# A transformer block's hand-written instruction order, moved in small steps, with key and value products cut in two

## The chip, the cores and the metric

The kernel runs on one core of one Trainium2 chip. The metric is the device time of one execution in microseconds; the kernel before was run three times.

## The reference

A pre-layernorm block with linear attention and a dense layer, on 2048 tokens of 640 values in bf16:

```python
h  = x + A(layernorm(x));   h2 = h + B(layernorm(h))
# A: q, k, v = split(x @ wqkv), 32 heads of 20
pq = einsum("bhsd,hdf->bhsf", q, w_phi);  pk = einsum("bhsd,hdf->bhsf", k, w_phi)
phi_q = concat([softmax(pq), softmax(-pq)]);  phi_k = concat([softmax(pk), softmax(-pk)])
kv  = einsum("bhsf,bhsd->bhfd", phi_k, v);    z = sum over s of phi_k
num = einsum("bhqf,bhfd->bhqd", phi_q, kv);   den = einsum("bhqf,bhf->bhq", phi_q, z) + 1e-6
out = (num / den) @ wo
# B: silu(x @ w1) @ w2, 640 -> 1728 -> 640
```

## The kernel before

The 2048 tokens are 16 tiles of 128. One string, `ORDER`, lists every step of the program. A word such as `kp.9@0` is an operation, its token tile, and the PSUM bank it starts at; a last letter names the engine that does it (`v` VectorE, `a` ScalarE, `p` GpSimd, `s` a DMA on SyncE's queue). The loop at the end of the kernel calls `op_kp(9)` and so on in this order, and each engine runs its own instructions strictly in the order of the string. Nothing is reordered later, so the string is the schedule: waits between engines come from the data, and from PSUM banks and buffers that are used again.

The first half works tile by tile:

- `wt`, `wc` transpose the key weight in five pieces and copy them out of PSUM; `ph` forms the block-diagonal map of w_phi from `phr` and `mask5`; `fk`, `fc` fold that map into the key weight (`Wfk`), so that one product gives the mapped keys. `lq`, `gk`, `gc` do the same for the queries (`Wfq`), with a transposing DMA in place of `wt`.
- `st`, `rs` are the statistics of a token tile and 1/sqrt of its variance (the power on GpSimd); `xn` normalises the tile, and `xt`+`xc` (PE and a copy) or `xd` (a DMA) transpose it into `XnT`.
- `kp` and `vp` are the key and value products, ten matmuls of 320 columns each through `proj`; `ke` takes both exponentials of the keys on ScalarE, `kr` their sums and reciprocals on VectorE, `kn` the division (`p` all on GpSimd, `q`, `b`, `d` shared, `v` all on VectorE); `vc` copies the values out. `cc` adds the tile to the state, which stays in bank 7 until all 16 are in; `kc`, `km` then write it out masked.
- `qp`, `qs`, `qr`, `qt` are the four parts of a query product on four token tiles, and `qe` its exponentials.

The second half reads the state out: `dp` (40 small matmuls, four banks), `dw`, `dr`, `do` (weights, reciprocal, and two halves of the output `o`), `td` (a transposing DMA), `op` (output projection), `oa` (residual added), `sq`, `sr`, `hn`, `hd` (second layernorm and a transposing DMA into `HnT`), then per group of two or four tiles `up`, `ua` (first dense product, silu) and `yp`, `yh`, `yo` (second product, its last half-row, and residual with the store). `lx`, `lk`, `lv`, `lo`, `l1`, `l2`, `lh`, `lp` load tokens, weights and w_phi. `wm` are matmuls of ones, run at the start while nothing has landed.

Lines that the prediction uses: L169 and L171 are all copies out of PSUM (VectorE, ScalarE); L198 is `ph`; L236 all plain loads; L268 `wm`; L273 and L274 `st`; L278 and L281 `rs`; L297 and L302 `xn`; L308 `xt`; L322 `wt`; L337 `fk` and `gk`; L370 `proj`; L395 `ke`; L403 and L406 `kr`; L414 and L418 `kn`; L427 `cc`; L457 the query products; L479 `qe`; L504 `dp`; L539 `do`; L559 `td`; L566 `op`; L605 and L613 `hn`; L630 `hd`; L645 and L655 `up`; L691 `yp`; L704 `yh`.

Of the kernel before, what the change touches and what calls it, by code (L numbers as in the profile page):

```python
# [30 lines left out]
lx.12.16.s vp.1@6 st.10 xt.2@5 vp.0@0 xc.2.a xn.9.a vc.0.a vp.2@2 st.11 lo.2.5.s xn.3.v xt.3@4 xc.3.a  # L31
rs.10.12 xn.8.a vc.2.a vc.1.a kp.2@0 ke.2 st.4 xd.9 st.5 kp.3@4 lo.0.2.s ke.3 rs.4.6 vp.3@2 xn.11.v vp.9@6
vc.9.a xn.4.a kp.9@0 ke.9 vc.3.a st.12 st.13 st.6 rs.12.14 xd.8 kr.1 kn.1.p kp.8@4 ke.8 mc.1 xn.13.a xn.12.a
xd.11 vp.11@6 vp.8@0 vc.8.a xn.5.v kr.0 kp.11@2 lq.2.s ke.11 st.7 rs.6.8 xn.6.a st.14 st.15 rs.14.16 xd.4
kr.9 vp.4@4 vc.4.a xd.5 vp.5@0 kn.0.p vc.11.a kr.2 vc.5.a kn.9.p kp.5@2 kr.11 kn.11.p gk.2@4 xn.10.a gc.2.a
xd.12 vp.12@6 vc.12.v kr.3 kn.3.p kp.4@0 xn.15.a ke.4 kp.12@4 cc.9 cc.1 kr.4 kn.4.p cc.0 xn.14.v cc.11 ke.5
kr.5 kn.2.d xd.13 ke.12 kr.12 lq.4.s xd.6 kp.6@0 lq.0.s ke.6 vp.13@2 vc.13.a kp.13@4 ke.13 vp.6@0 xd.15
xd.10 gk.4@2 vp.10@4 vc.6.a lq.3.s gk.3@0 gc.4.a gc.3.a vc.10.a kn.5.q kp.10@2 kn.12.p kr.6 xn.7.a l1.3.s
kn.6.q lq.1.s gk.1@0 gc.1.a kr.13 kn.13.p cc.4 cc.5 l1.0.s ke.10 kr.10 cc.2 cc.3 cc.12 xd.14 xd.7 kr.8
kn.8.p kn.10.d vp.15@4 vc.15.a kp.15@0 ke.15 kp.14@2 gk.0@4 gc.0.a vp.7@0 ke.14 kr.14 kn.14.p qp.0.1@4  # L40
qs.0.1 qr.0.1 kp.7@2 ke.7 l2.10.13.s kr.15 l1.2.s cc.8 vc.7.v cc.13 l2.2.4.s cc.10 qt.0.1 qp.0.0@2 qs.0.0
kn.15.p qr.0.0 qt.0.0 qe.0.1 l2.4.6.s kr.7 kn.7.v l2.6.8.s qe.0.0 vp.14@0 vc.14.a qp.0.2@6 qs.0.2 cc.6 cc.7
mt qe.0.2 cc.15 cc.14 kc km.0 lh.s qp.3.0@4 qs.3.0 qr.3.0 km.1 dp.0@0 l1.4.s close dw.0.p dr.0 qt.3.0
do.0.1.p qe.3.0 qp.2.0@6 qs.2.0 qr.2.0 qt.2.0 qe.2.0 do.0.0.p dp.1@0 dw.1.p qp.1.0@4 dr.1 do.1.0.p qs.1.0
qr.1.0 qt.1.0 qe.1.0 qp.1.1@6 td.0 do.1.1.p td.1 dp.3@0 dw.3.p dr.3 do.3.0.p qs.1.1 qr.1.1 qt.1.1 qe.1.1
qp.3.2@4 qp.1.2@5 dp.2@0 dw.2.p qs.1.2 qe.1.2 do.3.1.p td.3 qs.3.2 op.0@6 dr.2 do.2.1.p do.2.0.p qe.3.2 oa.0
dp.4@0 dw.4.p td.2 sq.0 qp.2.2@5 qs.2.2 qe.2.2 op.1@6 oa.1 sr.0 qp.2.1@4 dp.6@0 dw.6.p l1.5.s l1.1.s qs.2.1
qr.2.1 hn.0.a hd.0 sq.1 qt.2.1 sr.1 hn.1.v hd.1 qe.2.1 op.3@6 oa.3 sq.3 dp.5@0 dw.5.p op.2@4 sr.3 oa.2
hn.3.a sq.2 dr.5 do.5.0.p do.5.1.p qp.3.1@6 qs.3.1 l2.0.2.s l2.8.10.s qr.3.1 dp.9@0 dw.9.p td.5 dr.9
do.9.0.p dr.6 do.6.1.p dr.4 do.4.1.p do.4.0.p td.4 qt.3.1 qe.3.1 up.0.2@4 ua.0.2 dp.7@0 sr.2 up.0.0@6 ua.0.0  # L50
dw.7.p dr.7 up.0.3@4 ua.0.3 do.6.0.p dp.8@0 dw.8.p dr.8 hn.2.a up.0.1@6 ua.0.1 td.6 do.8.0.p op.5@4 oa.5
dp.12@0 dw.12.p dr.12 yp.1.0@6 do.7.1.p do.7.0.p sq.5 td.7 hd.3 op.4@4 oa.4 sr.5 hn.5.v hd.5 do.9.1.p sq.4
td.9 sr.4 hn.4.a dp.10@0 dw.10.p yp.1.1 yp.0.1@4 yh.0.0 hd.2 hd.4 yo.1 dp.11@0 dw.11.p dr.11 do.8.1.p
do.11.0.p td.8 yp.0.0 yo.0 op.7@6 oa.7 sq.7 dr.10 op.6@0 oa.6 sq.6 sr.6 op.9@2 up.1.6@4 do.11.1.v td.11 oa.9
sq.9 dp.15@0 ua.1.6 sr.9 up.1.5@6 ua.1.5 up.1.1@4 hn.9.v hd.9 do.10.0.p dw.15.p dr.15 hn.6.v hd.6 op.8@6
# [12 lines left out]
"""

@with_exitstack  # L70
def kernel(
# [194 lines left out]
    def op_wm(n=512):  # L266
        one = nc.const_aps.tensor
        nc.tensor.matmul(mm1()[:, 0:n], one(1.0, (P, P), BF16), one(1.0, (P, n), BF16), start=True, stop=True)  # L268

    def op_st(t):  # L270
        stats = sm.tile([P, 2, 6], F32, name="stats")
        for k in range(2):
            nc.vector.bn_stats(stats[:, k, :], X[:, t, k * 320 : (k + 1) * 320])  # L273
        nc.vector.bn_aggr(MV[:, t, :], stats[:])  # L274

    def op_rs(a, b):
# [86 lines left out]
            tl["gk", ce][:, 1, 0:320].rearrange("p (k r f) -> p k r f", k=2, r=C),  # L363
        )

    def proj(t, W):
        ps = mm2()
        for c in range(C):
            for half in range(2):
                nc.tensor.matmul(  # L370
                    ps[:, half, 0:320], tok(XnT[t // GT], t)[:, c, :], W[:, c, half * 320 : (half + 1) * 320],
                    start=(c == 0), stop=(c == C - 1),
                )
# [384 lines left out]
```

## Time and profile before

| | us |
|---|---|
| median of three runs | 236.25 (236.18 to 236.31) |
| the profiled execution | 236.35 |
| its span in the profile | 234.4 |
| TensorE busy | 230.5 |
| VectorE, ScalarE, GpSimd busy | 133.5, 114.5, 95.4 |

The span is from the first to the last instruction of the profile; some 2 us of the execution lie around it. Times in the rows are from the start of the span. A row of a timeline gives the start, the busy time, the engine, the line, the operation, out<-in with shapes, the count of merged instructions, and in brackets the idle time before it and what ended it. A piece of the chain of waits gives start, length, engine and line. A row of the grouped view ends with busy time, the mean of one in ns, and the idle time before the group. A DMA row gives the size and the median time from issue to landing. A matmul's row counts its way through the array, so that matmuls that follow each other overlap in it; their pace is read from starts, or from the pieces of the chain.

### The profile page before, as it was taken

How to read it: one execution, taken by the hardware profiler on the slowest of the kernel's cores; microseconds unless marked ns; L12 is line 12 of the kernel's file. 1: busy time of each engine (PE TensorE's matmuls, PEld its weight loads, DVE VectorE, ACT ScalarE, POOL GpSimd, SP SyncE). 2: the span in 40 equal slices, each digit the busy share in tenths (PEclk: the TensorE clock that was granted, in tenths of full speed). 3: DMA queues.
4: the chain of work that ended last, by engine and by line, in shares of the span. 5: the costliest groups of instructions: out<-in, count | busy, mean ns of one | idle time of the engine just before them, and what ended most of it. 6: DMA issues, size and time to landing. Idle time of an engine off the chain costs nothing.

```text
span 234.4 us, 6307 instructions
## 1 busy us (share of the span) xinstructions
PE 230.5 (98%) x2674; PEld 148.4 (63%) x2674; DVE 133.5 (57%) x249; ACT 114.5 (49%) x171; POOL 95.4 (41%) x190
## 2 busy tenths in 40 slices
...
DMA packets 44844, 20.67 MB, mean 88 GB/s; under 512 B 34448, under 2 KB 44304, under 8 KB 44816
## 3 DMA queue, kind: packets, MB, share of 16 engines
...
## 4 chain that ended last, share of the span: by engine, by line
PE 98%; ACT 1%; DVE 0%; issue 0%
PE mm L691 24%; PE mm L645 24%; PE mm L370 19%; PE mm L457 10%; PE mm L566 9%; PE mm L504 3%; PE mm L268 2%; PE mm L427 2%; PE mm L337 1%; PE mm L655 1%; PE mm L704 1%; ACT EqT L479 1%; PE mm L322 1%; PE mm L308 0%; DVE ob L721 0%
## 5 line engine op out<-in xcount | busy, mean ns | idle before, releaser
L691 PE MATMUL mm<-w,shT 128*128 128x320 bf16 (+2 forms) x416 | 58.7, 299 | 0.0
L645 PE MATMUL mm<-HnT,w 128*128 128x512 bf16 (+1 forms) x325 | 58.6, 337 | 0.0
L691 PEld LDWEIGHTS <-shT 128*128 128x128 bf16 x416 | 39.6, 98 | 17.2 <-issue 1.1
L667 ACT ACTIVATE shT<-mm 128x1024 bf16<-128x1024 f32 (+2 forms) x29 | 27.6, 963 | 44.6 <-PE mm L645 43.1
L712 DVE TENSOR_TENSOR ob<-mm,X 128x640 bf16<-128x640 f32 x15 | 12.3, 819 | 62.3 <-PE mm L691 59.3
L645 PEld LDWEIGHTS <-w 128*128 128x128 bf16 x325 | 31.4, 98 | 23.2
L370 PEld LDWEIGHTS <-XnT 128*128 128x128 bf16 x320 | 30.8, 98 | 12.0
L414 POOL TENSOR_TENSOR Ek<-Ek,Sk 128x1280 bf16<-128x1280 bf16 (+2 forms) x15 | 32.9, 2217 | 4.0 <-DVE Sk L406 4.0
L539 POOL TENSOR_TENSOR o<-u,rd 128x320 bf16<-128x320 f32 x28 | 19.9, 727 | 22.9 <-DVE rd L533 16.4
L583 ACT ACTIVATE sq<-X 128x640 bf16<-128x640 bf16 x16 | 11.7, 732 | 28.3 <-DVE X L575 27.2
L566 PE MATMUL mm<-wo,ot 128*128 128x320 bf16 x160 | 23.9, 299 | 0.3 <-ACT EqT L479 0.3
L457 PE MATMUL mm<-XnT,Wfq 128*128 128x512 bf16 x100 | 23.8, 380 | 0.0
L370 PE MATMUL mm<-wv,XnT 128*128 128x320 bf16 x160 | 23.7, 299 | 0.0
L370 PE MATMUL mm<-Wfk,XnT 128*128 128x320 bf16 x160 | 23.5, 299 | 0.0
L395 ACT ACTIVATE Ek<-mm 128x640 bf16<-128x640 f32 x32 | 20.5, 714 | 6.0 <-PE mm L370 5.1
L403 DVE TENSOR_REDUCE Sk<-Ek 128x64 f32<-128x1280 bf16 x16 | 23.2, 1452 | 0.3 <-ACT Ek L395 0.3
L479 ACT ACTIVATE EqT<-mm 128x1024 bf16<-128x1024 f32 (+1 forms) x24 | 19.7, 879 | 4.9 <-PE mm L457 4.8
L575 DVE SCALAR_TENSOR_TENSOR X<-mm,X 128x640 bf16<-128x640 f32 x16 | 13.0, 818 | 15.4 <-PE mm L566 15.1
L566 PEld LDWEIGHTS <-ot 128*128 128x128 bf16 x160 | 15.7, 98 | 7.3 <-issue 0.2
L273 DVE BATCH_NORM_STATS2 stats<-X 128x6 f32<-128x320 bf16 x32 | 13.6, 467 | 3.8 <-DMA X<-in_A_x_dram 3.8
L457 PEld LDWEIGHTS <-Wfq 128*128 128x128 bf16 x100 | 9.1, 98 | 9.3
L525 DVE TENSOR_TENSOR u<-mm,w 128x672 f32<-128x672 f32 x16 | 13.7, 857 | 1.2 <-DVE w L523 0.3
...
## 6 DMA issues: line engine op xcount, KB each, us to landing
out_dram<-ob SPq DMA_DIRECT2D x15, 160.0 KB, 1.8
...
wk<-in_A_wqkv_dram SPq DMA_DIRECT2D x4, 160.0 KB, 4.2
...
```

Of the source, the lines that this page charges most:

```text
L370: nc.tensor.matmul(ps[:, half, 0:320], tok(XnT[t // GT], t)[:, c, :], W[:, c, half * 320 : (half + 1) * 320], start=(c == 0), stop=(c == C ...
L395: nc.scalar.activation(Ek[:, s, :].rearrange("p (a n) -> p a n", a=2), tl["kp", t][:, :, 0:320], AF.Exp, scale=1.0 - 2.0 * s,)
L403: nc.vector.tensor_reduce(Sk[:], tl["ek", t][:].rearrange("p s (h f) -> p (s h) f", f=DH), axis=AX.X, op=ALU.add,)
L414: nc.gpsimd.tensor_tensor(Ek3[:, 0:n], Ek3[:, 0:n], Sk[:, 0:n].unsqueeze(2).to_broadcast([P, n, DH]), op=ALU.mult,)
L457: nc.tensor.matmul(tl["qp", g, i][:, k, :], Wfq[:, c, r * P : (r + 1) * P], XnT[g][:, c, :], start=(c == 0), stop=(c == C - 1),)
L479: nc.scalar.activation(E[:, s, rs[0] : rs[-1] + 1, :], tl["qp", g, i][:, 0 : len(rs), :], AF.Exp, scale=1.0 - 2.0 * s,)
L525: nc.vector.tensor_tensor(u[:], A[1][:, :, :, 0:21], w[:].unsqueeze(3).to_broadcast([P, 4, 8, 21]), op=ALU.mult,)
L539: (nc.vector if eng == "v" else nc.gpsimd).tensor_tensor(tl["o", t][:, a * 320 : (a + 1) * 320].rearrange("p (h f) -> p h f", f=DH), tl["u ...
L566: nc.tensor.matmul(ps[:, half, 0:320], tl["ot", t][:, c, :], wo[:, c, half * 320 : (half + 1) * 320], start=(c == 0), stop=(c == C - 1),)
L645: nc.tensor.matmul(ps[:, i * W : (i + 1) * W], w1[:, c, fc * P : (fc + 1) * P], HnT[g][:, c, 0:W], start=(c == 0), stop=(c == C - 1), skip ...
L667: nc.scalar.activation(sh[:, a:b], tl["up", g, k][:, 0 : b - a], AF.Silu)
L691: nc.tensor.matmul(ps, shT[g][:, fc * W + i * P : fc * W + (i + 1) * P], w2[:, fc, a:b], start=first and fc == 0, stop=last and fc == FC - ...
```

## The change

All 622 words of `ORDER` are written anew as 670. The steps are the same ones, with these differences:

- `kp` and `vp` are cut in two: `kp`, `vp` do three of the five weight pieces (six matmuls), new words `kq`, `vq` the other two (four). A product's second part can stand behind other work.
- `st` is cut in two: new word `sa` does the first half of a tile's statistics, `st` the second half and the aggregate.
- The fifth piece of the key weight (`wt.4`) is transposed second, and the state products `cc` are grouped otherwise.
- `ph` goes from VectorE to GpSimd, behind the constants of the values (`mo`) and the mask (`mk`).
- Copies: `wc` 4, 2 on ScalarE and 0, 1, 3 on VectorE (before 0, 1 and 2, 3, 4); `xc.2` to VectorE, `vc.7`, `vc.12` to ScalarE; `xn` 2, 9, 12, 15 to VectorE and 3, 11, 14 to ScalarE; `hn` 5, 7, 8, 10, 11, 13, 14 to ScalarE and 3 to VectorE; eight halves of `do` from GpSimd to VectorE and two the other way; `kn` 2, 7, 10 to GpSimd alone, 5 shared half and half, 12 and 14 with a quarter on GpSimd.
- The loads of `wo` go from the first 18 us to behind `xd.14`; `l1` and `l2` stand in another order, and `lh` goes behind `td.7`.
- PSUM banks are given out anew; the read-outs `dp` use banks 4 to 7 where most used 0 to 3.

The start, and the parts of the order that the prediction speaks of:

```diff
-mk mo lx.0.1.a lk.0.1.s lp.a lx.1.2.s lk.4.5.a wm.512@7 wm.512@7 wm.512@7 wm.512@7 wm.512@7 wm.512@7
-wm.512@7 wm.512@7 wt.0@0 lk.1.2.s ta wc.0.a wm.256@2 wm.256@2 wm.256@2 wm.256@2 wm.256@2 wm.256@2 wt.1@1 wc.1.a st.0 rs.0.1
-ph.v fk.0@2 fc.0.a st.1 lk.2.3.s wt.2@4 wc.2.v lk.3.4.s wt.3@5 wc.3.v fk.1@6 fc.1.a rs.1.2 fk.2@0 fc.2.a
-lx.2.4.s xn.0.v lx.8.12.s wt.4@4 wc.4.v lv.0.3.s fk.3@2 fc.3.a xt.0@5 xn.1.v xc.0.v st.2 fk.4@6 fc.4.a
-rs.2.3 lv.3.5.s mc.0 xt.1@4 xc.1.a st.9 st.8 rs.8.10 lx.4.8.s st.3 rs.3.4 kp.0@0 ke.0 xn.2.a kp.1@2 ke.1
...
+lx.0.1.a sa.0 lk.0.1.s mo lp.a wm.512@7 wm.512@7 wm.512@7 wm.512@7 wm.512@7 wm.512@7 wm.512@7 wm.512@7
+wt.0@0 lx.1.2.s lk.4.5.a lk.1.2.s st.0 lk.2.3.s lk.3.4.s wm.256@2 wm.256@2 wm.256@2 wm.256@2 wm.256@2
+wm.256@2 wt.4@1 wt.1@2 mk ph.p rs.0.1 sa.1 st.1 ta wc.4.a wt.2@3 wc.2.a rs.1.2 lx.2.4.s wc.0.v fk.0@4 fc.0.a
+wt.3@6 wc.1.v fk.1@0 lx.8.12.s fk.2@2 xn.0.v xt.0@7 wc.3.v fk.3@4 xn.1.v fc.1.a lv.0.3.s xt.1@6 fc.2.a
+xc.0.v kp.0@0 sa.2 xc.1.a st.2 fk.4@2 fc.3.a sa.3 rs.2.3 st.3 kp.1@6 rs.3.4 xn.2.v fc.4.a kq.0 kq.1 lv.3.5.s
+ke.0 xt.2@4 sa.8 vp.0@2 vq.0 sa.9 vp.1@0 vq.1 st.8 st.9 rs.8.10 xc.2.v vp.2@4 vq.2 ke.1 sa.10 st.10 lx.4.8.s
...
+qp.0.0@0 ke.15 qs.0.0 l2.10.13.s qr.0.0 qt.0.0 qe.0.0 kr.13 kp.7@4 kq.7 kn.10.p cc.5 cc.10 xd.14 kn.4.p cc.4
+kp.14@0 kq.14 kr.12 ke.7 qp.0.1@4 qs.0.1 qr.0.1 kn.13.p cc.13 kr.15 cc.6 kn.15.p vc.15.a cc.15 ke.14 kn.12.d
+cc.12 vp.14@2 vq.14 qt.0.1 kr.7 kn.7.p cc.9 cc.7 kr.14 kn.14.d vc.14.a cc.14 qe.0.1 mt close qp.0.2@6 qs.0.2
+qp.2.0@0 kc km.0 qp.3.0@2 qs.3.0 km.1 qe.0.2 dp.0@4 l1.1.s qr.3.0 dw.0.p qt.3.0 qs.2.0 qr.2.0 l1.3.s qt.2.0
...
+dw.4.p qp.2.2@2 qs.2.2 qe.2.2 op.1@0 oa.1 td.3 qp.2.1@2 do.2.1.p td.2 sr.0 hn.0.a dp.6@4 l2.2.4.s hd.0
+qs.2.1 qr.2.1 sq.1 qt.2.1 qe.2.1 dw.6.p op.3@0 l1.4.s sr.1 hn.1.v hd.1 l2.0.2.s oa.3 sq.3 sr.3 dp.5@4 dw.5.p
+op.2@2 oa.2 dr.5 l2.4.6.s do.5.1.p qp.3.1@0 qs.3.1 qr.3.1 do.5.0.p dp.9@4 td.5 sq.2 qt.3.1 qe.3.1 dw.9.p
...
+do.8.0.p do.6.1.v op.5@2 oa.5 sq.5 do.7.0.p td.7 dp.12@4 dw.12.p dr.12 op.4@0 oa.4 lh.s yp.1.0@2 do.8.1.p
+td.8 dp.10@4 do.9.0.v yp.1.1 yp.0.1@0 td.6 sr.5 hn.5.a dw.10.p hd.5 yh.0.0 sq.4 yo.1 sr.4 dp.11@4 dw.11.p
...
+yp.14.0 yo.14 yp.15.1 yo.15 yp.13.0 yz.13.0.s yp.13.1 yz.13.1.a
...
+    def op_sa(t):
+        tl["stats", t] = sm.tile([P, 2, 6], F32, name="stats")
+        nc.vector.bn_stats(tl["stats", t][:, 0, :], X[:, t, 0:320])
+
     def op_st(t):
-        stats = sm.tile([P, 2, 6], F32, name="stats")
-        for k in range(2):
-            nc.vector.bn_stats(stats[:, k, :], X[:, t, k * 320 : (k + 1) * 320])
+        stats = tl["stats", t]
+        nc.vector.bn_stats(stats[:, 1, :], X[:, t, 320:D])
         nc.vector.bn_aggr(MV[:, t, :], stats[:])
...
-    def proj(t, W):
-        ps = mm2()
-        for c in range(C):
+    def proj(t, W, ps, cs):
+        for c in cs:
             for half in range(2):
...
     def op_vp(t):
-        tl["vp", t] = proj(t, wv)
+        tl["vp", t] = mm2()
+        proj(t, wv, tl["vp", t], range(3))
+
+    def op_vq(t):
+        proj(t, wv, tl["vp", t], range(3, C))
...
     def op_kp(t):
-        tl["kp", t] = proj(t, Wfk)
+        tl["kp", t] = mm2()
+        proj(t, Wfk, tl["kp", t], range(3))
+
+    def op_kq(t):
+        proj(t, Wfk, tl["kp", t], range(3, C))
```

More of the change, by code (lines that the diff above doesn't have):

```diff
@@ L31 @@
[L31 to L55, printed above, removed]
@@ new lines @@
+xc.0.v kp.0@0 sa.2 xc.1.a st.2 fk.4@2 fc.3.a sa.3 rs.2.3 st.3 kp.1@6 rs.3.4 xn.2.v fc.4.a kq.0 kq.1 lv.3.5.s
+ke.0 xt.2@4 sa.8 vp.0@2 vq.0 sa.9 vp.1@0 vq.1 st.8 st.9 rs.8.10 xc.2.v vp.2@4 vq.2 ke.1 sa.10 st.10 lx.4.8.s
+xn.9.v sa.11 st.11 vc.0.a sa.4 xn.3.a rs.10.12 mc.0 vc.1.a xn.8.a lx.12.16.s sa.12 xt.3@6 xc.3.a sa.7 kp.2@2
+kq.2 ke.2 xd.9 xd.8 vp.3@0 kp.3@6 lq.2.s xn.11.a kq.3 st.4 ke.3 vq.3 vc.3.a xd.11 vc.2.a kp.9@2 lq.3.s kq.9
+sa.5 sa.6 kp.8@6 st.5 rs.4.6 vp.8@0 xn.4.a vq.8 ke.9 sa.13 st.13 st.12 rs.12.14 xn.10.a xn.5.v vc.8.a st.6
@@ new lines @@
+st.7 mc.1 vp.9@4 kp.11@2 vq.9 kr.2 xn.12.v rs.6.8 xn.13.a xd.5 kq.11 ke.11 vc.9.a kn.2.p kr.3 kn.3.p vp.11@0
+kq.8 vq.11 ke.8 vc.11.a vp.5@2 vq.5 xn.6.a xd.4 vp.4@4 vq.4 kr.0 kn.0.p vc.5.a kr.1 xd.12 vc.4.a xn.7.a
+gk.2@6 kp.12@0 kq.12 vp.12@2 vq.12 gc.2.a kp.5@4 sa.14 kq.5 cc.0 vc.12.a st.14 cc.2 ke.12 xd.6 kp.6@2 vp.6@0
+vq.6 ke.5 vc.6.a kn.1.p kp.4@4 kq.6 kq.4 lq.0.s gk.0@0 cc.1 kr.11 kn.11.p ke.6 cc.11 kr.8 kn.8.p cc.8 ke.4
+sa.15 st.15 rs.14.16 kr.5 kn.5.b cc.3 kr.9 kn.9.p gc.0.a xd.10 l1.0.s kp.10@2 kq.10 ke.10 xd.13 xn.14.a
@@ new lines @@
+qp.2.0@0 kc km.0 qp.3.0@2 qs.3.0 km.1 qe.0.2 dp.0@4 l1.1.s qr.3.0 dw.0.p qt.3.0 qs.2.0 qr.2.0 l1.3.s qt.2.0
+dr.0 do.0.0.p dp.1@4 dw.1.p lo.0.2.s qe.3.0 dr.1 do.0.1.p do.1.0.p do.1.1.p qe.2.0 qp.1.0@2 qs.1.0 qr.1.0
+qt.1.0 qe.1.0 qp.1.1@0 lo.2.5.s dp.3@4 dw.3.p dr.3 do.3.1.p do.3.0.p qs.1.1 qr.1.1 l1.5.s qt.1.1 qp.1.2@2
+qp.3.2@3 dp.2@4 dw.2.p dr.2 qs.3.2 qs.1.2 qe.1.1 qe.1.2 td.0 op.0@0 td.1 oa.0 qe.3.2 sq.0 dp.4@4 do.2.0.p
+dw.4.p qp.2.2@2 qs.2.2 qe.2.2 op.1@0 oa.1 td.3 qp.2.1@2 do.2.1.p td.2 sr.0 hn.0.a dp.6@4 l2.2.4.s hd.0
@@ new lines @@
+qs.2.1 qr.2.1 sq.1 qt.2.1 qe.2.1 dw.6.p op.3@0 l1.4.s sr.1 hn.1.v hd.1 l2.0.2.s oa.3 sq.3 sr.3 dp.5@4 dw.5.p
+op.2@2 oa.2 dr.5 l2.4.6.s do.5.1.p qp.3.1@0 qs.3.1 qr.3.1 do.5.0.p dp.9@4 td.5 sq.2 qt.3.1 qe.3.1 dw.9.p
+dr.4 do.4.1.p l2.8.10.s do.4.0.p td.4 dr.9 up.0.2@2 ua.0.2 dp.7@4 l2.6.8.s dw.7.p up.0.0@0 ua.0.0 sr.2
+hn.2.a up.0.3@2 hn.3.v dp.8@4 hd.3 dr.6 do.6.0.v ua.0.3 up.0.1@0 dr.7 do.7.1.p dw.8.p hd.2 ua.0.1 dr.8
+do.8.0.p do.6.1.v op.5@2 oa.5 sq.5 do.7.0.p td.7 dp.12@4 dw.12.p dr.12 op.4@0 oa.4 lh.s yp.1.0@2 do.8.1.p
@@ new lines @@
+td.8 dp.10@4 do.9.0.v yp.1.1 yp.0.1@0 td.6 sr.5 hn.5.a dw.10.p hd.5 yh.0.0 sq.4 yo.1 sr.4 dp.11@4 dw.11.p
+dr.11 do.11.1.v yp.0.0 op.6@2 oa.6 hn.4.a do.9.1.p td.9 op.8@4 op.7@6 oa.8 sq.6 sr.6 op.9@2 oa.7 hd.4
+do.12.0.v sq.8 sr.8 hn.6.v hd.6 oa.9 yo.0 do.11.0.v sq.9 td.11 up.1.5@4 ua.1.5 sr.9 hn.9.v hd.9 hn.8.a sq.7
+sr.7 hn.7.a hd.7 dp.14@0 up.1.2@6 up.1.1@4 ua.1.1 ua.1.2 dw.14.p dr.14 up.1.3@0 ua.1.3 dr.10 up.1.6@2
+do.10.0.v do.14.1.v dp.15@4 up.1.4@0 ua.1.6 ua.1.4 dw.15.p dr.15 hd.8 up.2.6@2 ua.2.6 do.12.1.p dp.13@4
```

26 lines of the change are left out of this document (12 added, 14 removed).

## The prediction

> **What bounds the kernel now.** I read the page first (span, busy shares), then the chain of work that ended last, then the timelines of single engines over the first 13 us, where alone TensorE (PE) is not full.
>
> ```profile
> span 234.4 us, 6307 instructions
> PE 230.5 (98%) x2674; PEld 148.4 (63%) x2674; DVE 133.5 (57%) x249; ACT 114.5 (49%) x171; POOL 95.4 (41%) x190
> ...
> 4.94 1.28 PE mm L268 x6
> 6.25 0.45 PE mm L322 x5
> 6.70 0.32 PE mm L337 x6
> 8.96 0.28 PE mm L308 x5
> 38.20 1.32 PE mm L427 x128
> 45.38 1.36 PE mm L370 x10
> 65.20 1.13 PE mm L427 x128
> 68.37 2.91 PE mm L457 x13
> 71.68 2.70 PE mm L457 x12
> ...
> 88.29 1.52 PE L566 MATMUL mm<-wo,ot 128*128 128x320 bf16 x10 [0.27 <-ACT EqT L479]
> ```
>
> The first two lines are the page's, the rest are pieces of the chain, and the last is from PE's timeline. The chain is matmuls nearly from end to end, at their own pace: ten of 320 columns take 1.36 us, 136 ns each. So an order can win only where PE waits, or by fewer changes of tile shape, and it can lose wherever a producer comes late. The last line holds the only wait of PE for an engine after the start, 0.27 us. What can be won is this and part of the first 10 us.
>
> **The start.** Up to the second key product the same matmuls stand in both orders: five transposes of the key weight (wt), five products with the block map (fk), two token transposes (xt), two key products. Before, all are issued by 12.72:
>
> ```profile
> 1.70 0.56 ACTq L236 DMA_DIRECT2D wk<-in_A_wqkv_dram  x1
> wk<-in_A_wqkv_dram ACTq DMA_DIRECT2D x1, 160.0 KB, 4.3
> 5.00 0.15 DVE L278 TENSOR_SCALAR RS<-MV 128x1 f32<-128x1 f32 x1
> 5.08 0.99 DVE L198 TENSOR_TENSOR phb<-phr,mask 128x800 bf16<-128x800 bf16 x1
> 7.33 0.89 DVE L169 COPY wTk<-mm 128x640 bf16<-128x640 bf16 x2 [0.22 <-PE mm L322]
> 8.20 0.44 DVE L297 TENSOR_SCALAR xn<-X,MV,RS 128x640 bf16<-128x640 bf16 x1
> 9.45 0.48 DVE L169 COPY XnT<-mm 128x640 bf16<-128x640 bf16 x1
> 6.74 0.69 ACT L171 COPY wTk<-mm 128x640 bf16<-128x640 bf16 x1 [1.07 <-PE mm L322]
> 7.33 3.17 ACT L171 CAST Wfk<-mm 128x640 bf16<-128x640 f32 x5
> 12.72 0.71 PE L370 MATMUL mm<-wv,XnT 128*128 128x320 bf16 x4
> ```
>
> VectorE's queue led to 10 us: statistics, block map (0.99), three weight copies, two normalisations, XnT at 9.45 to 9.93. After, the map leaves VectorE and the copies stay three (pieces 0, 1, 3). With the statistics of token 1 at 5.1 in place of the map, wc.0 comes at 6.3, wc.1 6.8, xn.0 7.25, wc.3 7.7, xn.1 8.15, xc.0 8.6 to 9.1, a gain of 0.85 at most. The fifth piece lands at 1.70 + 4.3 = 6.0, 0.25 ahead of piece 1, and takes PE from the warm-up there; pieces 1 and 2 follow, and fk.0 can go at 6.85, when wc.0 is done.
>
> ScalarE then holds the end: wc.4 (at 6.0 + 0.49, the distance from 6.25 to 6.74), wc.2, fc.0, fc.1, fc.2, xc.1, fc.3, fc.4. At 0.59 a weight copy (6.74 to 7.33), 0.61 an fc (3.17 over five) and 0.6 for xc.1, fc.4 ends at 6.5 + 1.2 + 3.05 + 0.6 + 0.1 = 11.45. As the products are cut after three of five weight pieces, kp.0 needs only fc.2 and starts at 9.2 to 9.9; fk.4 (0.32), kp.1 and the first part of kq.0 fill the time to fc.4. The last 0.27 of kq.0 and the 0.54 of kq.1 come after it, so PE is through at 12.3, or 12.8 if the normalisations come late. The floor is PE without a pause from 6.0: 4 x 0.28 + 5 x 0.33 + 2 x 0.28 + 2 x 1.36 = 6.05, so 12.1. Against 12.72: **-0.6 to +0.1, I take -0.2**, as three engines have to meet.
>
> The map on GpSimd has no row. The nearest, with those of its input:
>
> ```profile
> 1.22 0.45 ACTq L236 DMA_DIRECT2D phr<-in_A_w_phi_dram  x1
> phr<-in_A_w_phi_dram ACTq DMA_DIRECT2D x1, 25.0 KB, 3.6
> L414 POOL TENSOR_TENSOR Ek<-Ek,Sk 128x960 bf16<-128x960 bf16 x2 | 3.9, 1942 | 0.0
> L414 POOL TENSOR_TENSOR Ek<-Ek,Sk 128x320 bf16<-128x320 bf16 x2 | 2.4, 1178 | 0.0
> ```
>
> On the line between 320 and 960 columns, 800 make 1.75 us, from 4.9 (1.22 + 3.6, and a start) to 6.65, 0.2 ahead of need. Between 1.2 and 1.95 by the two rows themselves, it is late by nothing that matters. Queued behind it on GpSimd are the powers for tokens 0 and 1, and xn.0 waits for the first; that is the 12.8 above.
>
> **Tile shapes.** One matmul more in a stretch of L457 costs 0.21 (2.91 against 2.70), so 12 are 2.52 and 0.18 is left for entering and leaving small tiles. The state products (cc) stood in four groups, of which the first and the last are quoted (L427); read off the new order they make five: 0+2, 1+11+8+3, 5+10+4, 13+6+15+12, 9+7+14. The read-outs (dp) and half-row groups (yh) keep their count. **+0.2.** The cuts of kp, vp and the statistics add no instruction: 0.
>
> **The wait at 88 us stays.** The new order has again qt.2.1, op.3, dp.5, then op.2 in the banks that qe.2.1 frees (2 in place of 4): 0 taken, -0.27 at best.
>
> **12 to 68 us.** The products rotate through PSUM banks that ScalarE frees. It gets two value copies more, one token copy and one xn less, so no new load. The tightest place is the end. From the end of qt.0.0 to the last state product, cc.14, PE has 3 x 1.36 of products, 2.15 of query work, nine cc at 0.28 (1.13 for four) and three entries into small tiles of 0.2: 9.3 in all. The chain beside it:
>
> ```profile
> 60.65 1.94 ACT L479 ACTIVATE EqT<-mm 128x1024 bf16<-128x1024 f32 x2 [0.32 <-PE mm L457]
> 59.03 1.30 ACT L395 ACTIVATE Ek<-mm 128x640 bf16<-128x640 f32 x2 [2.43 <-PE mm L370]
> L403 DVE TENSOR_REDUCE Sk<-Ek 128x64 f32<-128x1280 bf16 x16 | 23.2, 1452 | 0.3 <-ACT Ek L395 0.3
> L406 DVE RECIPROCAL Sk<-Sk 128x64 f32<-128x64 f32 x16 | 8.8, 553 | 0.6
> L414 POOL TENSOR_TENSOR Ek<-Ek,Sk 128x1280 bf16<-128x1280 bf16 x11 | 26.9, 2456 | 4.0 <-DVE Sk L406 4.0
> 55.45 3.14 POOL L414 TENSOR_TENSOR Ek<-Ek,Sk 128x1280 bf16<-128x1280 bf16 x1 [1.42 <-DVE Sk L406]
> ```
>
> 0.3 (a matmul's end to the next engine) + 1.94 (qe.0.0) + 1.30 (ke.7) + 2.0 (kr.7) + 2.46 (kn.7, now on GpSimd) + 1.18 (GpSimd's quarter of kn.14) = 9.2, on time by 0.1. With a kn of 3.14 it is 0.6 late. **0 to +0.6, I take +0.1.**
>
> **After 68 us** the read-out stage repeats the old order with its banks mirrored (dp in 4 to 7 in place of 0 to 3). Net six hn move from VectorE to ScalarE, and net six halves of do from GpSimd to VectorE, about one short operation there for another.
>
> ```profile
> L613 ACT ACTIVATE hn<-X,hm 128x640 bf16<-128x640 bf16 x6 | 5.5, 921 | 8.1 <-POOL hm L610 8.1
> 83.47 1.15 SPq L236 DMA_DIRECT2D w<-in_B_w_dram  x2
> 103.80 1.76 SPq L559 DMA_TRANSPOSE ot<-o  x1
> w<-in_B_w_dram SPq DMA_DIRECT2D x2, 80.0 KB, 5.6
> 110.00 0.38 PE mm L704 x4
> ```
>
> ScalarE: 6 x 0.92 = 5.5 us, hidden by PE's products, as ScalarE is busy only 49%; uncovered, each hn would cost its 0.92. On SyncE's queue the wo loads leave the first 18 us for a place behind xd.14, far ahead of op.0: 0. The fourth w1 slice now stands between hd.0 and hd.1 and may hold hd.1, which token group 0 awaits, by one issue: 0 to 0.57. The tail load lh goes behind td.7 (103.8 and one transpose, so 105) and lands by 110.6 at the latest; yh.0.0 asks for it at 110.0: 0 to 0.6. I take 0 for both, as each has other loads' company in its long row and little here. The last two projections and stores are unchanged: 0.
>
> **Sum.** -0.2 + 0.2 + 0.1 = +0.1. The profiled execution has a span of 234.4 in 236.35, so 234.5 and 236.45; the median of the runs, 236.25, lies 0.1 below it: **236.3**.
>
> **Rivals.** *Slower: the map holds VectorE's port.* While GpSimd forms the map from two SBUF tiles (4.9 to 6.65), VectorE's small add for RS at 5.0, and all queued behind it, would wait.
>
> ```profile
> 14.11 0.72 POOL L281 TENSOR_TENSOR RS<-RS,nhalf 128x2 f32<-128x2 f32 x1
> 14.21 0.15 DVE L278 TENSOR_SCALAR RS<-MV 128x1 f32<-128x1 f32 x1
> 40.24 0.77 DVE L297 TENSOR_SCALAR xn<-X,MV,RS 128x640 bf16<-128x640 bf16 x1
> ```
>
> Against: that add ran in 0.15 inside a GpSimd operation. For: an xn took 0.77 in place of 0.44 while GpSimd normalised keys. If all is held to 6.65, XnT is ready at 10.6 and PE through the set at 10.6 + 0.32 + 2.72 = 13.65, 0.9 later; with the tile shapes +1.1, **237.4**. It decides once the add waits more than 0.7.
>
> The Trainium skill ("SBUF — State Buffer", Who interferes with whom) has the shared port pair locked for a whole instruction, the other engine fully blocked. By that rule 237.4 would come out; the rows at 14 us speak against it for so small an add.
>
> I give this rival 0.15, and a late producer elsewhere (cc.14, hd.1, lh) at +0.6, 236.9, another 0.15.
>
> *Faster: PE runs without a pause from 6.0 and ScalarE is early at 88 us.* -0.6 + 0.2 - 0.27 = -0.7: **235.6**. For it: the early fifth piece, and VectorE relieved by 1 us. Against: ScalarE's eight copies follow each other without slack. Chance 0.24.
>
> **Numbers.** The forecast's case, within 0.2% (0.47 us, about what a measurement of this kernel can tell from no change), has 0.46; slower by more 0.30; faster by more 0.24. The range runs from the faster rival's 235.6 to just under the port rival, 237.3; beyond its ends lie about half of the faster case's chance and half of the port's.
>
> **What would show it.** Right: the first value product begins at 12.3 to 12.8, the stretch of L457 behind the first dp (68.37 before) within 0.5 of its old time, five L427 groups in the chain, and a wait near 0.3 at 88. The port: the second token's statistics after 6 us and the first key product after 10.3. The prediction is wrong if PE waits more than 0.5 us in one place after 13 us, or if the first 13 us gain over 0.6.

## Result and profile after

| | us | against the kernel before |
|---|---|---|
| before, median of 11 runs | 236.27 (236.13 to 236.6) | |
| after, median of 11 runs | 236.96 (236.61 to 238.2) | 1.0029, 95% interval 1.0018 to 1.0041 |
| profiled execution after | 237.15, span 235.4 | before 236.35, span 234.4 |

The change costs 0.69 us, 0.29%: inside the range, but outside the 0.2% of the forecast's own case. Of the profile after, first the page's head, then pieces of its chain of waits (start, length, what), then the waits of PE for other engines and transfers (total, times, longest):

```profile
span 235.4 us, 6297 instructions
PE 228.6 (97%) x2655; PEld 148.1 (63%) x2674; DVE 130.7 (56%) x247; ACT 119.2 (51%) x177; POOL 95.1 (40%) x192
```

```profile
1.72 4.77 DMA wk<-in_A_wqkv_dram
6.53 1.01 PE mm L327 x15
...
58.19 1.31 ACT Ek L406 x2
59.59 1.50 DVE Sk L414
61.11 0.56 DVE Sk L417
61.83 1.82 POOL Ek L425
63.65 0.49 issue
64.14 1.65 POOL Ek L425
65.84 0.38 PE mm L438 x32
...
69.47 2.75 PE mm L468 x12
```

```profile
PE mm L327 <- DMA wk<-in_A_wqkv_dram: 0.9, 1, 0.9
...
PE mm L577 <- ACT EqT L490: 0.3, 1, 0.3
```

The line numbers moved: L327 is `wt` (322 before), L374 `proj` (370), L438 `cc` (427), L468 the query products (457), L414 and L417 `kr`, L425 and L429 `kn`, L577 `op` (566), L656 `up` (645). PE shows 2655 of 2674 matmuls, so the page's 97% is a little low, and gaps of a whole matmul are missing records, not waits. Eleven of the missing ones are query matmuls (L468, 89 of 100), among them the first one behind the last state product and the first one behind the first read-out.

The stretch behind the first read-out (`dp`) starts at 69.47, against 68.37 before: 1.1 later, of which some 0.2 is a missing first record. The read-out itself starts 0.96 later (68.84 against 67.88, rows below), and the span is 1.0 longer. So all of it is lost before 69 us and nothing after. Two places show in the chain. PE waits at the start for the fifth key piece, and the end of the state stage hangs on the key chain: exponential (L406), sum and reciprocal on VectorE (L414, L417), two divisions on GpSimd (L425), last state product (L438). Before, the chain ran through matmuls here. (The 0.49 of "issue" is the rest of tile 7's division: GpSimd's timeline has it from 61.83 to 64.18.)

### The profile page after: what moved, and what is told of

Its sections match the earlier page's. It is cut to its first block, busy times and chain, and to the rows that moved or that the text cites. A ratio compares the mean times of both kernels' runs of the same rounds, so it can differ in the third digit from the quotient of the medians.

```text
span 235.4 us, 6297 instructions
## 1 busy us (share of the span) xinstructions
PE 228.6 (97%) x2655; PEld 148.1 (63%) x2674; DVE 130.7 (56%) x247; ACT 119.2 (51%) x177; POOL 95.1 (40%) x192
## 4 chain that ended last, share of the span: by engine, by line
PE 82%; DVE 9%; ACT 3%; DMA 2%; POOL 1%; issue 1%; ACTq 0%; DVEq 0%; POOLq 0%
PE mm L702 24%; PE mm L656 24%; PE mm L374 10%; PE mm L577 9%; PE mm L468 7%; DVE Sk L414 5%; PE mm L515 3%; DMA wk<-in_A_wqkv_dram 2%; DVE Sk L417 2%; ACT Ek L406 2%; POOL Ek L425 1%; DVE Ek L429 1%; PE mm L666 1%; PE mm L715 1%; PE mm L342 1%
## 5 line engine op out<-in xcount | busy, mean ns | idle before, releaser
L656 PE MATMUL mm<-HnT,w 128*128 128x512 bf16 (+1 forms) x318 | 58.3, 336 | 0.4
L656 PEld LDWEIGHTS <-w 128*128 128x128 bf16 x325 | 31.3, 98 | 23.8 <-issue 0.2
L723 DVE TENSOR_TENSOR ob<-mm,X 128x640 bf16<-128x640 f32 x15 | 12.3, 824 | 59.7 <-PE mm L702 48.6
L374 PEld LDWEIGHTS <-XnT 128*128 128x128 bf16 x320 | 30.6, 98 | 12.1 <-issue 0.4
L425 POOL TENSOR_TENSOR Ek<-Ek,Sk 128x1280 bf16<-128x1280 bf16 (+3 forms) x16 | 34.4, 2173 | 3.3 <-DVE Sk L417 3.2
L550 POOL TENSOR_TENSOR o<-u,rd 128x320 bf16<-128x320 f32 x22 | 16.0, 745 | 28.0 <-DVE rd L544 20.2
L414 DVE TENSOR_REDUCE Sk<-Ek 128x64 f32<-128x1280 bf16 x16 | 23.2, 1452 | 2.9 <-ACT Ek L406 2.9
L374 PE MATMUL mm<-Wfk,XnT 128*128 128x320 bf16 x160 | 24.5, 299 | 0.0
L374 PE MATMUL mm<-wv,XnT 128*128 128x320 bf16 x160 | 24.0, 299 | 0.2 <-issue 0.2
L577 PE MATMUL mm<-wo,ot 128*128 128x320 bf16 x160 | 23.4, 299 | 0.3 <-ACT EqT L490 0.3
L468 PE MATMUL mm<-XnT,Wfq 128*128 128x512 bf16 x89 | 22.0, 379 | 1.2 <-issue 1.0
L406 ACT ACTIVATE Ek<-mm 128x640 bf16<-128x640 f32 x32 | 20.6, 707 | 2.8 <-PE mm L374 2.6
L577 PEld LDWEIGHTS <-ot 128*128 128x128 bf16 x160 | 15.6, 98 | 7.0 <-issue 0.2
L624 ACT ACTIVATE hn<-X,hm 128x640 bf16<-128x640 bf16 x12 | 10.9, 918 | 11.2 <-POOL hm L621 11.1
L468 PEld LDWEIGHTS <-Wfq 128*128 128x128 bf16 x100 | 9.1, 98 | 9.5
```

The source lines that it names most:

```text
L374: nc.tensor.matmul(ps[:, half, 0:320], tok(XnT[t // GT], t)[:, c, :], W[:, c, half * 320 : (half + 1) * 320], start=(c == 0), stop=(c == C ...
L406: nc.scalar.activation(Ek[:, s, :].rearrange("p (a n) -> p a n", a=2), tl["kp", t][:, :, 0:320], AF.Exp, scale=1.0 - 2.0 * s,)
L414: nc.vector.tensor_reduce(Sk[:], tl["ek", t][:].rearrange("p s (h f) -> p (s h) f", f=DH), axis=AX.X, op=ALU.add,)
L425: nc.gpsimd.tensor_tensor(Ek3[:, 0:n], Ek3[:, 0:n], Sk[:, 0:n].unsqueeze(2).to_broadcast([P, n, DH]), op=ALU.mult,)
L468: nc.tensor.matmul(tl["qp", g, i][:, k, :], Wfq[:, c, r * P : (r + 1) * P], XnT[g][:, c, :], start=(c == 0), stop=(c == C - 1),)
L550: (nc.vector if eng == "v" else nc.gpsimd).tensor_tensor(tl["o", t][:, a * 320 : (a + 1) * 320].rearrange("p (h f) -> p h f", f=DH), tl["u ...
```

## Experiments

All times are medians with the ratio to the kernel before in runs on the same chip, and the 95% interval of the ratio; the changed kernel itself stands at 1.0029 and, repeated, 1.0027. Of all variants only k2, k4 and e5 have intervals clear of the changed kernel's (1.0018 to 1.0041), so everything smaller rests on the profiles, one for each variant.

### The kernel once more

> The changed kernel once more, nothing altered: a second profile of it. If the time behind the prediction lies in the order itself, the ratio is 1.002 to 1.004 again, the fifth key piece is awaited until about 6.5 us, the five groups of small-tile products return, and the pauses inside the group at 41.9 us (0.43 us), in the second matmul of the last value product (0.33) and before the last state product (0.29) return at the same places within 0.1 us. If those pauses are chance (a transfer, code arriving late), at least one of them is gone or elsewhere by more than 0.2 us and the ratio moves with it.

237.04 us, 1.0027 (1.0013 to 1.004). PE's timeline, repeated kernel first, then after (start, busy, bracket: idle before and for what):

```profile
6.01 1.28 PE L327 MATMUL mm<-ident,wk 128*128 128x128 bf16 x15
...
12.51 0.44 PE L313 MATMUL mm<-ident,xn 128*128 128x128 bf16 x5
...
68.36 0.47 PE L515 MATMUL mm<-KVBD,EqT 32*128 32x44 bf16 x40
```

```profile
6.53 1.01 PE L327 MATMUL mm<-ident,wk 128*128 128x128 bf16 x15 [0.93 <-DMA wk<-in_A_wqkv_dram]
...
12.76 0.44 PE L313 MATMUL mm<-ident,xn 128*128 128x128 bf16 x5
...
68.84 0.47 PE L515 MATMUL mm<-KVBD,EqT 32*128 32x44 bf16 x40
```

This time the fifth piece was there when the warm-up ended at 6.01, and the set of transposes, folds and key products was through at 12.51, not 12.76. So half of the 0.52 by which the piece came late in the first profile was chance that reached the end. From there to the read-out both take about the same, 55.85 and 56.08; before it took 55.16 (from 12.72 to the row below, PE's timeline of before). That part, 0.7 to 0.9 longer, belongs to the order.

```profile
67.88 0.49 PE L504 MATMUL mm<-KVBD,EqT 32*128 32x44 bf16 x40
```

### The start: which piece first

```diff
-wt.4@1 wt.1@2        (k1)      -lp.a ... lk.4.5.a       (k2)
+wt.1@2 wt.4@1                  +... lk.4.5.a lp.a
```

> Only the order of two transposes of the key weight is turned: piece 1, which landed at 6.18 us, ahead of the fifth, which landed at 6.49. Theory A, the start is bound by PE, which stands in order behind the late piece: PE leaves the warm-up at 6.2, and all behind it is 0.28 us earlier (time 0.3 below the changed kernel's). Theory B, the start is bound by ScalarE's eight copies, of which the first needs the fifth piece in either order (6.5 + 0.49): the last of the products' copies still ends at 11.9, the two key products still end at 12.7 to 12.8, and the time is the changed kernel's within 0.1 us.

> Only the load of the fifth key piece goes ahead of that of the feature weight on ScalarE's queue, about 0.5 us earlier. If its late landing is what cost the forecast gain, it lands by 6.0, ScalarE's first copy starts at about 6.5 in place of 7.0, the two key products end at 12.2 to 12.4 in place of 12.76, and the time falls by 0.3 to 0.5 us against the changed kernel. The price could be the map, whose input then lands up to 0.6 later: if the map ends after 7.0, the first product with it is late and the gain is under 0.15. If the landing does not matter, the time stays within 0.1 us.

Piece 1 first: 237.0 us, 1.0027 (1.0015 to 1.0038), no gain. It doesn't decide between its theories, as in its profile no piece was late. The fifth piece's load ahead: 238.1 us, 1.0069 (1.0057 to 1.0082). The price named came in full, and more:

```profile
6.49 1.52 POOL L200 TENSOR_TENSOR phb<-phr,mask 128x800 bf16<-128x800 bf16 x1 [2.13 <-DMA phr<-in_A_w_phi_dram]
8.06 0.47 PE L342 MATMUL mm<-phb,wTk 128*128 128x140 bf16 x6 [1.32 <-POOL phb L200]
```

With the load of w_phi behind that of the fifth piece on ScalarE's queue the map starts at 6.49 in place of 4.66, and PE waits 1.32 us for it. The piece was never the only thing that the start hung on.

### The map back on VectorE, and the cut undone

```diff
-mk ph.p rs.0.1        (k4)     -xc.0.v kp.0@0 sa.2 xc.1.a st.2 fk.4@2 fc.3.a ... fc.4.a kq.0 kq.1     (e10)
+mk ph.v rs.0.1                 +xc.0.v fk.4@2 fc.3.a fc.4.a sa.2 kp.0@0 kq.0 xc.1.a ... kp.1@6 kq.1
```

> Only the block map goes back from GpSimd to VectorE, where it took 0.99 us before. If GpSimd's map does not hold VectorE up, as the profile suggests (the small add ran in 0.15 us at 4.95, inside the map's 1.52), VectorE's first seven steps come about 1 us later: the first key product starts 0.4 to 0.9 us later than 9.72, and the time rises by 0.3 to 0.9 us against the changed kernel. If GpSimd's map held VectorE's port (the slower rival of the forecast), taking it away from GpSimd gives time back: equal or up to 0.5 us faster.

> Undoes the cut of the first two key products: as before, the fourth and fifth folded pieces and both their copies come ahead of the whole first key product, and the copy of the second token behind them. If the cut earns what the forecast says (the first part needs three of five pieces), the first key product starts about 1.2 us later (11.4 to 11.9 in place of 9.5 to 9.7), the two key products end 0.6 to 1.2 us later, and the time rises by 0.4 to 1.2 us. If PE would have been bound elsewhere, below 0.2.

The map on VectorE: 237.86 us, 1.0059 (1.0045 to 1.0073). The rows are those of this kernel, then two of the kernel after:

```profile
5.08 0.95 DVE L200 TENSOR_TENSOR phb<-phr,mask 128x800 bf16<-128x800 bf16 x1
7.77 0.49 PE L342 MATMUL mm<-phb,wTk 128*128 128x140 bf16 x6 [0.66 <-DVE wTk L171]
10.04 0.99 PE L374 MATMUL mm<-Wfk,XnT 128*128 128x320 bf16 x6
```

```profile
4.66 1.52 POOL L200 TENSOR_TENSOR phb<-phr,mask 128x800 bf16<-128x800 bf16 x1 [0.30 <-DMA phr<-in_A_w_phi_dram]
4.95 0.15 DVE L283 TENSOR_SCALAR RS<-MV 128x1 f32<-128x1 f32 x1
5.02 0.48 DVE L274 BATCH_NORM_STATS2 stats<-X 128x6 f32<-128x320 bf16 x1
```

VectorE's weight copy is late by 0.66 and the first key product starts 0.3 to 0.6 later than in the two profiles of the change. With the map on GpSimd, VectorE's add took its 0.15 us and a statistics step 0.48 inside the map's 1.52. The slower rival falls: in this profile GpSimd's map held nothing up.

The cut undone: 237.22 us, 1.0042 (1.0029 to 1.0055), some 0.2 to 0.3 us more than with the cut, less than expected and within the intervals. In its profile the key products began at 9.82 all the same, as their first matmuls need only the first pieces, and PE waited inside them for the later copies:

```profile
9.82 3.07 PE L374 MATMUL mm<-Wfk,XnT 128*128 128x320 bf16 x20
12.73 0.44 PE L313 MATMUL mm<-ident,xn 128*128 128x128 bf16 x5
```

The products end at 12.73. With the cut, in the four profiles that had no piece late and the same start (the repeat, e5, e7 and e11), they end at 12.31 to 12.52: the cut earns 0.2 to 0.4.

### The end of the state stage

```diff
-kr.7 kn.7.p cc.9 cc.7 kr.14 kn.14.d vc.14.a cc.14 qe.0.1 mt close
+kr.7        cc.9 cc.7 kr.14         vc.14.a cc.14 qe.0.1 mt close       (e6)
+mt kr.7 kn.7.p cc.9 cc.7 kr.14 kn.14.v vc.14.a cc.14 qe.0.1 close       (e8)
```

> Leaves out the division of key tiles 7 and 14 by their sums (kn.7 and kn.14); everything else stays. Theory A, the end of the state stage is bound by the key chain (exponential, sum, division on GpSimd, the last quarter): from the start of the last value product to the end of the last state product PE took 3.80 us in every profile so far, of which 0.68 is pause; without the two divisions it takes 3.1 to 3.2 and the time falls by 0.6 to 0.7 us, to the kernel before. Theory B, the pauses are PE's own (instructions that come late): the 0.2 to 0.66 us in the second matmul of the last value product stays, only the rest goes, and the time falls by 0.1 to 0.4.

> The division of key tile 14 goes wholly to VectorE (GpSimd had a quarter of it, queued behind the division of tile 7), and the transposition of the mask goes ahead of it into a pause of VectorE. Chain now: GpSimd's quarter ends 1.65 us after tile 7's division. If GpSimd is the late one, the last state product starts 0.15 to 0.5 us earlier and the time falls by as much. If VectorE alone is slower with the whole tile (1.92 us for 1280 columns once before, against 1.47 for 960 now), it starts at the same time within 0.1 us or later, and nothing is gained.

Without the two divisions 236.55 us, 1.0015 (1.0002 to 1.0028); with the last one on VectorE 236.86, 1.0024 (1.0012 to 1.0037). (e6 leaves out two divisions, so its output is not the block's; it only prices the chain.) PE's timeline from the last value product to the first read-out, parts of it, after, then e6, then e8:

```profile
62.57 0.31 PE L374 MATMUL mm<-wv,XnT 128*128 128x320 bf16 x1
63.05 1.38 PE L374 MATMUL mm<-wv,XnT 128*128 128x320 bf16 x9 [0.17 <-issue]
65.01 0.66 PE L438 MATMUL mm<-Ek,Vp 128*21 128x40 bf16 x64
65.84 0.38 PE L438 MATMUL mm<-Ek,Vp 128*21 128x40 bf16 x32 [0.17 <-POOL Ek L425]
66.37 1.46 PE L468 MATMUL mm<-XnT,Wfq 128*128 128x512 bf16 x6 [0.16 <-issue]
...
68.84 0.47 PE L515 MATMUL mm<-KVBD,EqT 32*128 32x44 bf16 x40
```

```profile
62.35 1.66 PE L374 MATMUL mm<-wv,XnT 128*128 128x320 bf16 x10
...
68.14 0.47 PE L515 MATMUL mm<-KVBD,EqT 32*128 32x44 bf16 x40
```

```profile
62.01 1.62 PE L374 MATMUL mm<-wv,XnT 128*128 128x320 bf16 x10
65.03 0.37 PE L438 MATMUL mm<-Ek,Vp 128*21 128x40 bf16 x32 [0.16 <-DVE Ek L429]
...
68.03 0.47 PE L515 MATMUL mm<-KVBD,EqT 32*128 32x44 bf16 x40
```

From the first row of each to its last: 6.27, 5.79 and 6.02; in the repeat it is 6.27 too (62.09 to 68.36). So the key chain costs 0.48, and 0.25 of that goes when VectorE takes the whole of tile 14. The 3.80 of the expectation, and the 0.47 that e11's expectation takes from e8, are too large by one matmul: they run to the first query row, and in the profile of after that row lacks its first record (11 query matmuls are listed up to the read-out, 12 in e6 and e8). In e7, e9 and e10, where the record is there, the same stretch is 3.57 to 3.58, against 3.09 in e6 (62.35 to 65.44) and 3.33 in e8.

The medians fell by 0.4 and by 0.1 to 0.2, near the 0.48 and 0.25 and less than the 0.6 to 0.7 that the first theory named. The pause inside the value product (63.05, 0.34 behind its place) cost nothing in after: it varies from 0.1 to 0.7 between the profiles, and with the chain as in after the stretch stays 6.26 to 6.32, since PE has to wait at product 14 anyway.

Why the chain is longer than forecast shows in GpSimd's quarters of a tile. The first two rows are the two of the kernel before, the others tile 14 in after, GpSimd's quarter and VectorE's part:

```profile
58.55 0.72 POOL L414 TENSOR_TENSOR Ek<-Ek,Sk 128x320 bf16<-128x320 bf16 x1
43.19 1.64 POOL L414 TENSOR_TENSOR Ek<-Ek,Sk 128x320 bf16<-128x320 bf16 x1
64.14 1.64 POOL L425 TENSOR_TENSOR Ek<-Ek,Sk 128x320 bf16<-128x320 bf16 x1
63.73 1.47 DVE L429 TENSOR_TENSOR Ek<-Ek,Sk 128x960 bf16<-128x960 bf16 x1
```

The quarter takes 0.72 when VectorE divides nothing meanwhile, and 1.64 when it does (VectorE's division ran from 42.91 to 44.24 beside the one at 43.19). A whole tile on GpSimd shows the same: 2.35 alone, 3.27 in after at 57.02, where VectorE's division of another tile ran until 58.08. In each case the one that starts second is longer by about the time that the other still runs: GpSimd's quarter at 64.14 by 0.92, with 1.06 of VectorE's division left.

### Small matmuls in a row

```diff
-kq.5 cc.0 vc.12.a st.14 cc.2 ke.12 ... vq.6 ke.5 vc.6.a kn.1.p kp.4@4 kq.6 kq.4 lq.0.s gk.0@0 cc.1 kr.11 ... cc.3
+kq.5      vc.12.a st.14      ke.12 ... vq.6 ke.5        kn.1.p kp.4@4 kq.6 kq.4 lq.0.s cc.0 vc.6.a cc.2 cc.1 kr.11 ... cc.3 gk.0@0   (e5)
+kq.5 cc.0 vc.12.a kn.1.p st.14 cc.2 cc.1 ke.12 ... vq.6 ke.5 vc.6.a   kp.4@4 kq.6 kq.4 lq.0.s gk.0@0      kr.11 ... cc.3   (e9)
```

> State products 0 and 2 move behind the products of token 6 into the group of 1, 11, 8 and 3, so that PE enters small tiles four times in place of five; one key tile more is buffered, one copy of a value tile and one query weight product move behind the group. If the fifth group costs what the forecast took, the profile has four groups and the time falls by 0.15 to 0.25 us against the changed kernel (ratio to the kernel before 1.002). If entering is free or covered by a producer that is late anyway (the last state product waits for the key chain, 0.68 us in all), the group disappears and the time stays within 0.1 us, with a longer pause at the end of the stage.

> State product 1 moves from the second group (1, 11, 8, 3) into the first (0, 2), with its division ahead; five groups stay, of 96 and 96 small matmuls in place of 64 and 128. Theory A, the pauses of 0.04 to 0.43 us inside the second group, and the stop of 3.56 us in the run with 192 small matmuls in one group, come from PE's instructions, which arrive in blocks of 16 KB while 256 of them pass in 1.13 us: a shorter group runs without a pause, and its stretch is 0.85 plus 0.1 us; time 0.05 to 0.3 below the changed kernel. Theory B, the pauses are for a producer of product 8 or 3: they stay, at the same clock time, and the time stays within 0.1 us.

Four groups: 240.51 us, 1.0187 (1.0155 to 1.0218), 3.5 us slower, which neither theory had. Product 1 in the first group: 236.8 us, 1.0017 (1.0007 to 1.0027). The chain of e5, then the DMA queues of e5 between 43.6 and 44.6 us (its only packet of the instruction queue between 41 and 47):

```profile
40.73 1.81 PE mm L438 x164
42.54 3.39 issue
45.93 0.35 PE mm L438 x28
```

```profile
q8 instruction: 1, 0.02, 5.8%
```

PE stops in the middle of one state product and no engine is late. PE's instructions come over a queue of their own, q8, in blocks: the page of after counts 21 packets and 0.34 MB there, so 16 KB each, and the 2674 matmuls with as many weight loads make some 255 instructions for each block. In e5 the next block started at 43.60, 1.1 us after PE had stopped and 2.3 us before it went on; in after the same block, the third of the profile, started at 40.15, before the long group began at 41.93. The same distance stands elsewhere. Here are the DMA queues of after between 60 and 61.2 us (40 slices of 0.03 us; the digit is the 23rd, 60.66), then PE in e11 and in e12 (both below), whose blocks started at 61.08 and 60.85:

```profile
DMA  0000000000000000000000900000000000000000
q8 instruction: 1, 0.02, 5.3%
```

```profile
61.91 0.31 PE L374 MATMUL mm<-wv,XnT 128*128 128x320 bf16 x1
63.42 1.38 PE L374 MATMUL mm<-wv,XnT 128*128 128x320 bf16 x9 [1.21 <-issue]
```

```profile
61.93 0.58 PE L374 MATMUL mm<-wv,XnT 128*128 128x320 bf16 x3
63.13 1.11 PE L374 MATMUL mm<-wv,XnT 128*128 128x320 bf16 x7 [0.61 <-issue]
```

After: 60.66 to 63.05 is 2.39; e11: 61.08 to 63.42 is 2.34; e12: 60.85 to 63.13 is 2.28; e5: 43.60 to 45.93 is 2.33. The longest is 2.98, in k2 (60.87 to 63.85). In e12, whose start has two matmuls fewer, the pause comes two matmuls later, behind the third of the product: it keeps its place in PE's program, not in the work. So the pauses that the profile calls "issue" behind and inside long groups of small matmuls are PE waiting for its program. The 192 small matmuls of e5 used it up; the 128 of after lie at the edge. With 96 in the second group, e9's took 1.01 us, against 1.56 in after and 1.35 in the repeat for 128, of which 0.28 is the product that left; so 0.1 to 0.3 of pause went in the profile, which the median can't confirm. The Trainium skill ("Runtime: NRT & Kernel Launch", Instruction fetch mechanics) has the stream refilled in blocks of 16 KiB, 256 instructions, at a cost "mostly hidden". The size agrees; that it is hidden does not hold where 64 instructions pass in 0.28 us. What the extra group costs by itself no run isolates, since e5's stop covers it. An estimate from after: a key product takes 1.36 from its start to that of the next one, and 1.45 ahead of a group (56.11 to 57.56), so entering costs some 0.1.

### The wait at 93 us, and both repairs together

```diff
-dp.6@4 l2.2.4.s hd.0 ... op.3@0 l1.4.s sr.1 hn.1.v hd.1 l2.0.2.s oa.3
+dp.6@4 hd.0 ... op.3@0 sr.1 hn.1.v hd.1 l2.0.2.s oa.3     (e7; the two loads behind l1.5; e11, e12: the other four l2 loads from 83 to 95 us, too)
-... wm.256@2 wm.256@2 wt.4@1 wt.1@2                        (e12, with the tail of e8 and the group of e9)
+... wt.1@2 wt.4@1
```

> Two weight loads (the fifth w1 slice and a w2 slice) leave their places on SyncE's queue before and between the transposes of the normalised tokens 0 and 1 for a place some 25 us earlier. If these loads are what made the second transpose land 3.1 to 5.7 us after its issue, against which PE waited 0 to 1.06 us at 93 us, it lands within 2.6 to 3.2, there is no wait at 93 us, the slowest runs (238 us and over) are gone, and the median falls by 0.1 to 0.3. If they are not, the landing still varies by more than 1 us and the median stays within 0.1.

> The last division on VectorE as in e8 (0.47 us of the pause at 64 to 66 us in its profile), and all loads of w1 and w2 that stood among the transposes from 83 to 95 us some 20 us earlier. Sum by the profiles: changed kernel 236.8 to 237.0, less 0.45 for the tail, less 0.1 to 0.2 for the waits at 93 us that some executions have: 236.2 to 236.4, the kernel before within 0.1%. If the transpose of token 1 lands late for another reason than the loads, some executions stay 0.3 to 1 us longer and the median at 236.6.

> As e11, with product 1 in the first group as in e9, two warm-up matmuls fewer and key piece 1 ahead of the fifth. Where the pieces land by 5.7 us, PE takes them up at 5.6 to 5.7 in place of 6.0. Sum: e11's 236.3, less 0.05 to 0.3 for the second group, less 0 to 0.3 at the start: 235.8 to 236.2, faster than the kernel before by 0.05 to 0.4 us. If the loads or the clock after a shorter warm-up take back the start, and the group's pauses come back elsewhere, 236.3.

e7: 236.69 us, 1.0015 (1.0005 to 1.0025). e11 (tail of e8, loads early): 237.19, 1.0032 (1.002 to 1.0044). e12: 236.67, 1.0014 (1.0002 to 1.0026). None beats the kernel before. First PE in e9, then the DMA issues of e9 and of e12 at 88 us (the last number is the time from issue to landing of the second token's transpose):

```profile
93.98 2.23 PE L656 MATMUL mm<-HnT,w 128*128 128x256 bf16 x19 [0.56 <-DMA HnT<-hn]
```

```profile
HnT<-hn SPq DMA_TRANSPOSE x1, 5.4
```

```profile
HnT<-hn SPq DMA_TRANSPOSE x1, 2.6
```

The same line has 4.3 before, 3.1 in after, 4.7 in the repeat, 5.7 in k4, 4.5 in e7 and 2.6 in e11. So among weight loads the transpose takes 3.1 to 5.7 us, alone 2.6; the first dense product wants it some 4.8 after its issue, so some executions wait (0.56 us in e9, 0.85 in e6, 0.90 in k4) and others not at all. The profile puts the waits in e6 and k4 down to a VectorE step, but in all three PE went on 0.13 to 0.14 after the transpose had landed. Moving only the two loads in front (e7) left one right behind, and 4.5. With all loads away (e11, e12) it is 2.6 and the wait is gone.

But the loads then run until about 61 us, where the next instruction block is due. e8 has the same end of the state stage with the loads at their old place: there the block started at 59.91, and PE paused 0.1 in the last value product. In e11 it started at 61.08, PE waits 1.21 us as shown, and with the key chain mended nothing covers that; in e12 it waits 0.61. e12's earlier start brought nothing either: PE took the pieces up at 5.89 and was through the key products at 12.46. So the sums in the expectations of e11 and e12 left out this wait, and both rest on 0.45 for the tail where 0.25 was to be had. No third place for the loads was tried.

## Why the prediction was right and wrong

- **The start, -0.2:** right in size where the fifth piece lands in time (12.51 against 12.72), +0.05 where it doesn't (12.76). Over all profiles that share this start the end lies from 12.24 (e8) to 12.96 (e9), with the piece landing from 5.7 to 6.7. The step took one landing, 6.0, for the landing. Its condition, three engines without slack, held, and PE was the one in front from 6.5 on. The cut earns 0.2 to 0.4 (e10); the map on GpSimd is what made the start possible (k4). The sign that the prediction named, a first value product at 12.3 to 12.8, reads 12.79 and 13.04, as a token transpose stands ahead of it.
- **The port rival:** excluded, by the test that the prediction named. The second token's statistics started at 5.02, not after 6. The prediction took the rule of the Trainium skill ("SBUF — State Buffer", Who interferes with whom) too broadly: by it a VectorE instruction with at most one SBUF input, outside the two-port modes, does not contend with GpSimd. The add and the statistics have one input each and ran in their usual 0.15 and 0.48. Where both engines divided, the later one took longer (1.64 in place of 0.72), and there the prediction did not look for it.
- **The fifth group, +0.2:** the five groups are there; by the estimate above each costs some 0.1.
- **The end of the stage, 0 to +0.6, taken as +0.1:** the step that missed; it is 0.48 (6.27 against 5.79). The mechanism was named and its term mis-sized. Chain, from the end of the query product (56.11) to product 14 (65.84) in after: 9.73, forecast 9.2. The difference is GpSimd's quarter of tile 14: from 64.14 to 65.84 is 1.7, where 1.18 was taken. That was the mean of 0.72 and 1.64, two quarters under different conditions, and the one that applied was 1.64. The other terms nearly cancel: the sum on VectorE is 0.24 longer (2.24 from start to GpSimd's start, 2.0 taken), the division of tile 7 0.15 shorter (2.31), the exponentials 0.06. PE's side was 9.73 - 0.48 = 9.25, forecast 9.3. So PE's sum was right, and one error of 0.5 in the chain turned "on time by 0.1" into 0.5 late.
- **The second group of `cc`:** not foreseen; 0.1 to 0.3 of pauses in the two profiles of the change, which the instruction blocks explain and e9 shortened. The rows held a sign of it: the two groups of 128 before took 1.32 and 1.13, and the prediction priced all by 1.13.
- **The wait at 88 us:** stays at 0.3, as said.
- **After 68 us, 0:** right in both profiles of the change. The 0 to 0.57 for `hd.1` was real, though, and too small at its end: 0 to about 1 us by the execution. The w1 slice before it (`l1.4`) is only a part of the cause.
- **The case:** what came was the late producer elsewhere, 236.9 with a chance of 0.15; measured 236.96. That the two agree to 0.1 is partly luck: the producer cost 0.48 and not 0.6, and the start and the pauses made up the rest. The forecast's own test, a stretch behind the first read-out within 0.5 of 68.37, failed in the profile after (the read-out 0.96 later) and just held in the repeat (0.48 later). Both sizes lie in the range, as its upper end was taken from the rivals.

The end of the stage (0.48) is shown by e6 and e8, the start by two profiles and k4, the wait at 93 us by e11 and e12. Of the 0.7 to 0.9 us by which the order is longer up to the read-out, 0.2 to 0.4 is left for the extra group and the pauses in the second one. How this, and the chance of the waits at 6 and 93 us, share in the median is open.
